# Releasing two granule loads by an average instead of a landed transpose, and moving the fourth block product by one step

## The chip, the cores and the metric

The kernel runs on one core of a Trainium2 chip. The core has a matrix engine (PE, with PEld for its weight loads), a vector engine (DVE), a scalar engine (ACT), GpSimd (POOL) and SyncE (SP, which here only issues transfers), and 16 DMA engines that move data between the device memory, called HBM in the profile, and the on-chip memory. Matrix results go to a small accumulation memory (PSUM) in which the kernel keeps pools of tiles. The metric is the device time of one execution in microseconds; lower is better.

## The reference

Attention with a sliding window and a few global keys, followed by a two-layer network. Shapes: batch 4, 8 heads, 768 positions, head size 64; the network has 3072 tokens, 512 features and 2048 hidden units.

```python
scores = scale * q @ k.T
keep = is_global | is_local            # 8 global keys, window of 96
scores = where(keep, scores - slope[h] * dist, -1e9)
a = softmax(scores);  x = a @ v        # x becomes 3072 x 512
h = x @ w_in
g = s * relu(h) ** 2 + b
out = g @ w_out
```

## The kernel before

**Granules and steps.** The 3072 tokens are cut into 12 granules of 256 tokens (two blocks of 128), three to a batch element. The attention of a granule is four units, one for each pair of heads. A *step* `s` (`step`, L956) handles units 2s and 2s+1, so granule j has the steps 2j and 2j+1. A step issues the score matmuls of step s+1 and their exponentials (ACT) and masks (DVE), then `stage_A` for its own two units: the average over the values on PE (L492), and the normalisation on DVE (reciprocal L462, product L463), which writes `xn[j]`. Between these it runs three lists of other work, `c0`, `c1` and `c2`, and a list `pre` ahead of the masks. The order on every engine is the order of the program text (`manual_schedule`); each engine works through its own queue, and waits come from the data and from tiles that are used again.

**From attention to the network.** When a granule's last step is done, `finish_granule(j)` (L947) turns `xn[j]` into `xT[j]`. From granule 4 on this is done by two DMA transposes from SP (L596). Then `hold_loads` (L120) puts a copy of one element on POOL, the *gate*: POOL's queue goes on only when that element is there. Behind it `load_granule(j + 4)` (L110) issues six loads of 128 KB on POOL (keys and queries into `nat`, L116, values into `vb`, L117, two blocks each; they cast from float32 to bf16). The keys and queries of granule j+2 are turned by DMA transposes as well (`qk_by_dma`, L357), which SP issues in the first of the two steps of granule j.

**The network.** The first matrix product of a granule is eight groups of 8 matmuls (`p1_mm`, L616), two groups to a *unit* `u1(j, q)`, q = 0 to 3: 16 matmuls of 128x256, a relu of each group (ACT, L626) and one square of the unit (ACT L792 or DVE L790). The second product of granules 4 to 11 is done for pairs (e, o) of granules with seven block products instead of eight (`product`, L816): sums and differences of hidden blocks (`g_sum`, L779) are multiplied by sums and differences of blocks of `w_out` (`weight_sums`, L750 to L753), and the results are joined on DVE (`evac` L825, `join` L864) and stored from SP. Each block product is 16 matmuls of 128x256, eight for each of the granule's two token blocks. The product numbers 1 to 7 name the operands; product 4 multiplies the second half of granule o's hidden units by the last weight difference, `t4`, which `weight_sums[3]` (L753) makes.

**The loop around the change.** The loop over pairs `pr` (L1149 to L1183) gives each pair four steps, from `k0 = 2e + 5`. In the kernel before, the third step runs the products 5 and 6, half sums, then product 4 (whose result is left in PSUM), then unit 0 of the next pair's granule e+2. The fourth step evacuates product 4 before the masks, runs product 3, and then units 1, 2 and 3 of granule e+2. `weight_sums[3]` closes the second step of the first such pair. The last pair (`tail`) has other lists in its third step.

**PSUM tiles of the network.** Products, `p1_mm` groups and others take tiles in turn from one pool of three (`ps_h`); a group or product can start when the result that lay in its tile three tiles ago has been read out. `stage_A` has a pool of one (`ps_av`).

Of the kernel before, what the change touches and what calls it, by code (L numbers as in the profile page):

```python
# [17 lines left out]
def kernel(  # L18
# [19 lines left out]
    DM = H * D  # L38
    DF = moe_w_in.shape[1]
    GB = 2  # L40
    GT = GB * P
# [78 lines left out]
    def hold_loads(ap):  # L120
        g = work.tile([P, 1], BF16, name="gate", tag="gate")
        nc.gpsimd.tensor_copy(g[0:1, :], ap)  # L122
# [144 lines left out]
    xn = {}  # L267
    xT = {}
# [324 lines left out]
    def x_by_dma(j):  # L593
        t = xT_tile(j)
        for i in range(GB):
            nc.sync.dma_start_transpose(t[:, :, i * P : (i + 1) * P], xn[j][:, i, :])  # L596
# [116 lines left out]
    def moe_p2_cols(j, tb, parts):  # L713
# [35 lines left out]
    weight_sums = [  # L749
        lambda: nc.vector.tensor_tensor(t1, w12, w11, ALU.subtract),  # L750
        lambda: nc.vector.tensor_tensor(t2, w22, t1, ALU.subtract),
        lambda: nc.vector.tensor_tensor(t3, w22, w12, ALU.subtract),
        lambda: nc.vector.tensor_tensor(t4, w21, t2, ALU.subtract),  # L753
    ]
# [3 lines left out]
    def quarter(j, half, c=None):  # L758
        lo, n = (0, NH) if c is None else (c * NH // 2, NH // 2)
        return g_of(j)[:, half * NH + lo : half * NH + lo + n, :]  # L760

    def g_sum(pr, n, c=None):

        def go():
            if pr not in gs_cur:
                gs_cur[pr] = [
                    gpool.tile([P, NH, GT], BF16, name="gsum", tag=f"gsum{i}", bufs=1)
                    for i in range(4)
                ]
            e, o = 2 * pr, 2 * pr + 1  # L770
            cs = slice(0, NH) if c is None else slice(c * NH // 2, (c + 1) * NH // 2)
            s1, s2, s3, s4 = (t[:, cs, :] for t in gs_cur[pr])
            dst, x, y, op = {
                1: (s1, quarter(o, 0, c), quarter(o, 1, c), ALU.add),
                2: (s2, s1, quarter(e, 0, c), ALU.subtract),
                3: (s3, quarter(e, 0, c), quarter(o, 0, c), ALU.subtract),
                4: (s4, quarter(e, 1, c), s2, ALU.subtract),
            }[n]
            nc.vector.tensor_tensor(dst, x, y, op)  # L779

        return go

    def unit_p1(j, q):

        for fp in (2 * q, 2 * q + 1):
            relu, _ = p1_mm(j, fp)
            relu()
        gs = g_of(j)[:, 4 * q : 4 * q + 4, :]
        if j % 2 or q == 3:
            outs.append(lambda: nc.vector.tensor_tensor(gs, gs, gs, ALU.mult))  # L790
        else:
            nc.scalar.activation(gs, gs, ACT.Square)  # L792
# [4 lines left out]
    def product(pr, n, tbs=range(GB), ps=None, cols=None):  # L797

        j = 2 * pr
        stat = {  # L800
            1: lambda: quarter(j, 0),
            2: lambda: quarter(j, 1),
            3: lambda: gs_cur[pr][3],
            4: lambda: quarter(j + 1, 1),
            5: lambda: gs_cur[pr][0],
            6: lambda: gs_cur[pr][1],
            7: lambda: gs_cur[pr][2],
        }[n]()
        mov = {1: w11, 2: w21, 3: w22, 4: t4, 5: t1, 6: t2, 7: t3}[n]
        cs = slice(0, CH) if cols is None else cols  # L810
        if ps is None:
            ps = ps_h.tile([P, GB, CH], F32, name="ps_2", tag="psh")
        prod_ps[pr, n] = ps
        for tb in tbs:
            for fc in range(NH):
                nc.tensor.matmul(  # L816
                    ps[:, tb, cs],
                    lhsT=stat[:, fc, tb * P : (tb + 1) * P],
                    rhs=mov[:, fc, cs],
                    start=(fc == 0),  # L820
                    stop=(fc == NH - 1),
                )

    def scaled(dst, ps, add):
        nc.vector.scalar_tensor_tensor(  # L825
            out=dst, in0=ps, scalar=s_bc[:], in1=add, op0=ALU.mult, op1=ALU.add
        )
# [6 lines left out]
    def both_blocks(ap):  # L834
        return ap.unsqueeze(1).to_broadcast((P, GB, CH))

    def put(pr, row, col, o, tb=None, c0=0, eng=nc.sync):

        b, g = divmod(2 * pr + row, NGR)
        t0 = b * S + g * GT  # L840
        cs = slice(col * CH, (col + 1) * CH)
        if tb is not None:
            t0 += tb * P
            c0 += col * CH
            eng.dma_start(out[t0 : t0 + P, c0 : c0 + o.shape[-1]], o)
        else:
            nc.sync.dma_start(out[t0 : t0 + GT, cs].rearrange("(a p) c -> p a c", p=P), o)
# [3 lines left out]
    def out_tile():  # L851

        n_out[0] += 1
        tag, bufs = (("first", 4), ("o_sb", 3))[n_out[0] % 2]
        return work.tile([P, GB, CH], F32, name="o_q", tag=tag, bufs=bufs)

    def store(pr, row, col, ps, add):

        o = out_tile()
        scaled(o[:].rearrange("p a c -> p (a c)"), ps, add)  # L860
        put(pr, row, col, o[:])

    def add_f32(dst, x, y):
        nc.vector.tensor_tensor(dst, x, y, ALU.add)  # L864

    def evac(pr, n):

        ps3 = prod_ps[pr, n][:]
        ps = ps3.rearrange("p a c -> p (a c)")
        if n == 1:  # L870
            res[pr] = [
                work.tile([P, GB, CH], F32, name=f"part{i}", tag=f"part{i}", bufs=1)
                for i in range(3)
            ]
            res[pr].append(out_tile() if pr == NJ // 2 - 1 else res[pr][0])
        r0, r1, r7, r6 = (t[:].rearrange("p a c -> p (a c)") for t in res[pr])
        if n == 1:
            scaled(res[pr][0][:], ps3, both_blocks(bvec[:, 0:CH]))
        elif n == 2:
            store(pr, 0, 0, ps, r0)  # L880
        elif n == 5:
            scaled(res[pr][1][:], ps3, both_blocks(bdiff[:]))
        elif n == 6:
            scaled(r6, ps, r0)
        elif n == 7:
            nc.scalar.activation(r7, ps, ACT.Copy, scale=s_bc[:])
        elif n == 3:
            store(pr, 0, 1, ps, r1)
        elif n == 4:
            store(pr, 1, 0, ps, r6)  # L890

    def join(pr, n):

        def go():
            _, r1, r7, r6 = (t[:].rearrange("p a c -> p (a c)") for t in res[pr])
            if n == 1:
                add_f32(r1, r1, r6)
            elif n == 0:
                add_f32(r6, r6, r7)
            else:  # L900
                o = out_tile()
                add_f32(o[:].rearrange("p a c -> p (a c)"), r7, r1)
                put(pr, 1, 1, o[:])

        return go

    def pe(pr, n):

        def go():
            product(pr, n)  # L910
            outs.append(lambda: evac(pr, n))

        return go

    def prod(pr, n):
        return lambda: product(pr, n)

    def u1(j, q):
        return lambda: unit_p1(j, q)

# [26 lines left out]
    def finish_granule(j):  # L947
        if j < X_PE:
            x_by_pe(j)
        else:  # L950
            x_by_dma(j)
        if 6 <= j + LEAD < NJ:
            hold_loads(xT[j][0:1, 0, GT - 1 : GT])
            load_granule(j + LEAD)

    def step(s, c0, c1, c2, pool=None, pre=()):  # L956
# [192 lines left out]
    for pr in range(2, NJ // 2):  # L1149
        e, o = 2 * pr, 2 * pr + 1  # L1150
        k0 = 2 * e + 5
        if k0 >= NU // 2:
            break
        step(
            k0,
            [pe(pr, 2)],
            [u1(o, 0)],
            [u1(o, 1), flush, g_sum(pr, 3, 0)],
            pre=[pe(pr, 1), flush],
        )  # L1160
        step(
            k0 + 1,
            [u1(o, 2)],
            [u1(o, 3), g_sum(pr, 1, 0)],
            [g_sum(pr, 1, 1), pe(pr, 7), g_sum(pr, 2)] + [weight_sums[3]] * (pr == 2),
            pre=[g_sum(pr, 3, 1)],
        )
        tail = k0 + 3 >= NU // 2
        step(
            k0 + 2,  # L1170
            [u1(e + 2, 0), pe(pr, 5)] if tail else [pe(pr, 5), flush, pe(pr, 6)],
            [pe(pr, 6), g_sum(pr, 4, 0)] if tail else [g_sum(pr, 4, 0), prod(pr, 4)],
            [g_sum(pr, 4, 1), u1(e + 2, int(tail)), join(pr, 1)],
        )
        if tail:
            break
        step(
            k0 + 3,
            [u1(e + 2, 1)],
            [join(pr, 2), u1(e + 2, 2)],  # L1180
            [u1(e + 2, 3)],
            pre=[join(pr, 0), lambda: evac(pr, 4), pe(pr, 3), flush],
        )  # L1183
    join(pr, 0)()
    for n in (3, 4):
# [4 lines left out]
    e, o = 2 * pr, 2 * pr + 1  # L1190
# [50 lines left out]
```

## Time and profile before

| | |
|---|---|
| median of 4 runs | 209.59 us (209.21, 209.48, 209.70, 209.76) |
| the profiled execution | 209.23 us, span 207.5 us |
| PE busy | 201.2 us (97%), granted clock 1.00 |
| DVE, ACT, POOL busy | 160.6, 128.5, 69.1 us |
| DMA | 28.17 MB in 110308 packets, of which 97836 under 512 bytes |
| queue of POOL's loads (q0) | 75472 packets, 13.11 MB |
| queue of SP's transfers (q1) | 33612 packets, 14.13 MB |
| transposes of xT, issue to landing | shortest 2.4, median 4.5, longest 9.2 us |

The page gives busy times and their shares by engine, then the span in 40 slices with the busy share in tenths, the chain of work that ended last, and the costliest groups of instructions. `L816` is line 816 of the kernel; `out<-in` names tiles. A matmul's duration in the profile includes the time in which it overlaps with the next one, so the pace of a run of matmuls is read from their starts. The steps of the first pair begin near 94.3, 102.4, 108.9 and 117.1 us, those of the second near 125.3, 133.4, 139.6 and 147.8 us.

### The profile page before, as it was taken

The page shows a single profiled execution, that of the slowest core. Times are in us where ns is not written, and L with a number is a line of the kernel's source. Part 1 is how long each engine was busy: PE and PEld are TensorE (multiplying, and loading weights), DVE is VectorE, ACT ScalarE, POOL GpSimd, SP SyncE. Part 2 cuts the span into 40 slices and gives each one's busy share as a digit, 9 for nine tenths or more (in the row PEclk, how much of TensorE's full clock was granted, in tenths as well). Part 3 has the DMA queues.
Part 4 walks back from the last instruction along what each step waited for, and adds up shares of the span by engine and source line. Part 5 has one row for each costly group of instructions (what it writes and reads, how often), then busy time and mean ns, then how long its engine had stood idle before and what let it go on. Part 6 is the DMA issues. An engine that isn't in the chain of part 4 may idle for free.

```text
span 207.5 us, 5323 instructions
## 1 busy us (share of the span) xinstructions
PE 201.2 (97%) x2191; PEld 159.9 (77%) x2191; DVE 160.6 (77%) x336; ACT 128.5 (62%) x200; POOL 69.1 (33%) x89
## 2 busy tenths in 40 slices
PE   6899999999999999999999999999999999999993
PEld 2677884556876685878888898888898889888883
DVE  7685689995989955799799974699865696737974
ACT  4975669484975648786564595664695764476200
POOL 8994244999737102703800917300000000000000
PEclk9999999999999999999999999999999999999999
DMA  6999999999999999999999999996460300240006
GB/s 166 171 180 206 206 208 174 155 152 136 118 149 153 155 159 173 93 240 247 140 207 130 126 145 178 205 202 79 53 205 3 89 17 0 52 153 0 0 6 200
DMA packets 110308, 28.17 MB, mean 136 GB/s; under 512 B 97836, under 2 KB 108780, under 8 KB 110284
## 3 DMA queue, kind: packets, MB, share of 16 engines
q0 software_dynamic: 75472, 13.11, 86.5%
q1 hardware_dynamic: 33612, 14.13, 39.4%
q10 hardware_dynamic: 1200, 0.59, 1.1%
q8 instruction: 17, 0.28, 0.6%
q14 instruction: 7, 0.06, 0.1%
HBM read 27.26 MB, written 6.29 MB: 162 GB/s over the span
## 4 chain that ended last, share of the span: by engine, by line
PE 82%; DMA 13%; POOL 4%; issue 0%; DVE 0%; POOLq 0%
PE ps L616 34%; PE ps L816 24%; PE ps L664 13%; DMA w_out_bf<-in_moe_w_out_dram 9%; PE ps_s L438 5%; PE ps_av L492 5%; DMA w_in_bf<-in_moe_w_in_dram 3%; POOL nat L102 2%; POOL vb L108 1%; PE ps_t L348 1%; PE ps_last L816 0%; PE ps_x L588 0%; POOL w_in_bf L140 0%; DVE o_last L825 0%; POOL rel L173 0%
## 5 line engine op out<-in xcount | busy, mean ns | idle before, releaser
L616 PE MATMUL ps<-xT,w_in_bf 128*128 128x256 bf16 x768 | 90.4, 273 | 0.5 <-DMA w_in_bf<-in_moe_w_in_dram 0.5
L626 ACT ACTIVATE gT<-ps 128x512 bf16<-128x512 f32 x96 | 55.7, 598 | 47.4 <-PE ps L616 47.1
L616 PEld LDWEIGHTS <-w_in_bf 128*128 128x128 bf16 x768 | 72.9, 98 | 10.0 <-DMA w_in_bf<-in_moe_w_in_dram 0.7
L447 ACT ACTIVATE pt<-ps_s 128x1024 bf16<-128x1024 f32 (+1 forms) x44 | 39.3, 946 | 3.1 <-PE ps_s L438 3.1
L664 PE MATMUL ps<-w_out_bf,gT 128*128 128x512 bf16 x128 | 29.8, 380 | 0.2 <-DMA w_out_bf<-in_moe_w_out_dram 0.2
L816 PEld LDWEIGHTS <-gsum 128*128 128x128 bf16 x256 | 24.2, 98 | 3.7 <-DVE gsum L779 0.5
L454 DVE TENSOR_TENSOR pt<-pt,tmpl 128x1024 bf16<-128x1024 bf16 (+1 forms) x40 | 24.5, 644 | 1.7 <-ACT pt L447 1.6
L790 DVE TENSOR_TENSOR gT<-gT 128x1024 bf16<-128x1024 bf16 x20 | 13.7, 687 | 11.7 <-ACT gT L626 11.7
L664 PEld LDWEIGHTS <-gT 128*128 128x128 bf16 x128 | 11.7, 98 | 13.5 <-issue 0.5
L463 DVE TENSOR_TENSOR xn<-ps_av,rc 128x256 bf16<-128x256 f32 x48 | 20.4, 425 | 1.7
L816 PEld LDWEIGHTS <-gT 128*128 128x128 bf16 x200 | 18.6, 98 | 2.3
L117 POOL DMA_DIRECT2D vb<-in_v_dram x20 | 18.2, 910 | 6.5 <-DMA nat<-in_k_dram 2.9
L116 POOL DMA_DIRECT2D nat<-in_k_dram x20 | 17.7, 886 | 7.9 <-DMA w_in_bf<-in_moe_w_in_dram 2.7
L116 POOL DMA_DIRECT2D nat<-in_q_dram x20 | 17.8, 891 | 6.7 <-DMA vb<-in_v_dram 2.5
L462 DVE RECIPROCAL rc<-ps_av 128x4 f32<-128x4 f32 x48 | 8.9, 186 | 12.2 <-PE ps_av L492 10.2
L492 PEld LDWEIGHTS <-pt 128*128 128x128 bf16 x320 | 14.4, 97 | 2.7 <-DVE xn L463 0.7
L629 DVE TENSOR_TENSOR gT<-gT 128x512 bf16<-128x512 bf16 x32 | 12.9, 420 | 3.6 <-ACT gT L626 3.3
L492 PE MATMUL ps_av<-vb,pt 128*128 128x65 bf16 x208 | 15.4, 193 | 0.0
L816 PE MATMUL ps<-w_out_bf,gsum 128*128 128x256 bf16 x128 | 15.3, 273 | 0.0
L816 PE MATMUL ps<-wsub,gsum 128*128 128x256 bf16 x128 | 15.1, 273 | 0.0
L122 POOL COPY gate<-xT 1x1 bf16<-1x1 bf16 x6 | 1.4, 237 | 40.0 <-DMA xT<-xn 38.9
L816 PE MATMUL ps<-w_out_bf,gT 128*128 128x256 bf16 x120 | 13.9, 273 | 0.0
(112 smaller groups left out, 222.6 us busy)
## 6 DMA issues: line engine op xcount, KB each, us to landing
out_dram<-o_q SPq DMA_DIRECT2D x15, 256.0 KB, 2.4
vb<-in_v_dram POOLq DMA_DIRECT2D x24, 128.0 KB, 7.4
nat<-in_k_dram POOLq DMA_DIRECT2D x22, 128.0 KB, 6.7
nat<-in_q_dram POOLq DMA_DIRECT2D x22, 128.0 KB, 7.3
w_out_bf<-in_moe_w_out_dram POOLq DMA_DIRECT2D x4, 512.0 KB, 17.2
w_in_bf<-in_moe_w_in_dram POOLq DMA_DIRECT2D x3, 512.0 KB, 11.0
out_dram<-o_sb SPq DMA_DIRECT2D x4, 256.0 KB, 6.0
out_dram<-o_early SPq DMA_DIRECT2D x4, 256.0 KB, 5.6
```

The costliest lines, as they stand in the source:

```text
L116: nc.gpsimd.dma_start(t[:, n, i, :, :], rows_of(srcs[n], b, sb))
L117: nc.gpsimd.dma_start(vbuf[b % 2][:, sb, :, 0:D], rows_of(v, b, sb))
L447: nc.scalar.activation(pt[:, :, 0:ncol], ps[:, :, 0:ncol], ACT.Exp, scale=QSCALE)
L454: nc.vector.tensor_tensor(pv, pv, m.rearrange("p h a c -> p h (a c)"), ALU.mult)
L463: nc.vector.tensor_tensor(dst, av[:, :, :, 0:D], rc[:].to_broadcast((P, 2, 2, D)), ALU.mult)
L492: nc.tensor.matmul(av[:, i, hi, 0 : D + 1], lhsT=pt[:, hi, c * P : (c + 1) * P], rhs=vv, start=(n == 0), stop=(n == len(terms) - 1),)
L616: nc.tensor.matmul(ps[:, i, :], lhsT=w_in_bf[:, kc, fc * P : (fc + 1) * P], rhs=xT[j][:, kc, :], start=(kc == 0), stop=(kc == KC - 1),)
L626: nc.scalar.activation(gs, ps[:], ACT.Relu)
L629: nc.vector.tensor_tensor(gs, gs, gs, ALU.mult)
L664: nc.tensor.matmul(po[:], lhsT=g_of(j)[:, fc, tb * P : (tb + 1) * P], rhs=w_out_bf[:, fc, :], start=(fc == 0), stop=(fc == FC - 1),)
L790: outs.append(lambda: nc.vector.tensor_tensor(gs, gs, gs, ALU.mult))
L816: nc.tensor.matmul(ps[:, tb, cs], lhsT=stat[:, fc, tb * P : (tb + 1) * P], rhs=mov[:, fc, cs], start=(fc == 0), stop=(fc == NH - 1),)
```

## The change

The gate of the loads that follow granules 4 and 5, those of granules 8 and 9, now copies an element of `xn` that the last normalisation writes, instead of an element of `xT` that the second transpose lands. The later gates stay on `xT`.

In the third step of a pair, unit 0 of granule e+2 moves from the end to the place of product 4, and unit 1 comes where unit 0 was. Product 4 goes to the fourth step, after product 3, with its evacuation issued like that of other products. The last weight subtraction moves from the end of the second step to the end of the third one, behind the join.

```diff
@@ finish_granule
         if 6 <= j + LEAD < NJ:
-            hold_loads(xT[j][0:1, 0, GT - 1 : GT])
+            if j in (4, 5):
+                hold_loads(xn[j][0:1, GB - 1, DM - 1 : DM])
+            else:
+                hold_loads(xT[j][0:1, 0, GT - 1 : GT])
             load_granule(j + LEAD)
@@ the loop over pairs, second step
-            [g_sum(pr, 1, 1), pe(pr, 7), g_sum(pr, 2)] + [weight_sums[3]] * (pr == 2),
+            [g_sum(pr, 1, 1), pe(pr, 7), g_sum(pr, 2)],
             pre=[g_sum(pr, 3, 1)],
@@ third step
             [u1(e + 2, 0), pe(pr, 5)] if tail else [pe(pr, 5), flush, pe(pr, 6)],
-            [pe(pr, 6), g_sum(pr, 4, 0)] if tail else [g_sum(pr, 4, 0), prod(pr, 4)],
-            [g_sum(pr, 4, 1), u1(e + 2, int(tail)), join(pr, 1)],
+            [pe(pr, 6), g_sum(pr, 4, 0)] if tail else [g_sum(pr, 4, 0), u1(e + 2, 0)],
+            [g_sum(pr, 4, 1), u1(e + 2, 1), join(pr, 1)] + [weight_sums[3]] * (pr == 2),
@@ fourth step
-            [u1(e + 2, 1)],
+            [pe(pr, 4)],
             [join(pr, 2), u1(e + 2, 2)],
             [u1(e + 2, 3)],
-            pre=[join(pr, 0), lambda: evac(pr, 4), pe(pr, 3), flush],
+            pre=[join(pr, 0), pe(pr, 3), flush],
```

The helper `prod(pr, n)`, which issued a product without its evacuation, is removed with its only use.

More of the change, by code (lines that the diff above doesn't have):

```diff
@@ L913, in pe @@
         return go
-    def prod(pr, n):
-        return lambda: product(pr, n)
     def u1(j, q):
```

## The prediction

> **What bounds the kernel now.** I read the page first (parts 1, 2 and 4), then the busy time by stage, then the chain in order of time where the diff touches the code, then the timeline of the gates, and last what the DMA queues moved beside each other.
>
> The page of the kernel before, parts 1, 2 and 4:
>
> ```profile
> PE 201.2 (97%) x2191; PEld 159.9 (77%) x2191; DVE 160.6 (77%) x336; ACT 128.5 (62%) x200; POOL 69.1 (33%) x89
> ...
> DMA  6999999999999999999999999996460300240006
> ...
> PE 82%; DMA 13%; POOL 4%; issue 0%; DVE 0%; POOLq 0%
> ```
>
> The matrix engine is busy for 97% of the span and carries 82% of the chain that ended last. The DMA part of the chain is the loading of weights before 34.7 us. The DMA engines are busy, too, until about slice 28 of 40 (145 us). The busy time by stage (window; its length, then busy us and instructions of PE, PEld, DVE, ACT, POOL; granted clock; DMA share; GB/s):
>
> ```profile
> 76.00:94.00 18.00, 18.00 (x188) 12.75 (x186) 13.86 (x32) 14.10 (x26) 5.43 (x7) 1.00 1.58 178
> 94.00:126.00 32.00, 32.00 (x387) 27.44 (x385) 27.24 (x50) 20.77 (x30) 11.40 (x15) 1.00 1.63 164
> ```
>
> In both stages that the diff touches PE has no idle time, at a granted clock of 1.00. The chain there (start, us, what):
>
> ```profile
> 109.51 3.72 PE ps L816 x32
> 113.23 0.24 PE ps_av L492 x8
> 113.47 1.75 PE ps L816 x16
> 115.22 0.24 PE ps_av L492 x8
> 115.46 1.75 PE ps L616 x16
> 117.21 0.55 PE ps_s L438 x16
> 117.76 1.85 PE ps L816 x16
> 119.61 1.75 PE ps L616 x16
> ```
>
> This is the third step of the first pair (from 108.95 us) and the start of its fourth. A product of 16 matmuls and one unit of the first MoE product of 16 matmuls take the same 1.75 us, or 109 ns a matmul. So PE runs back to back: what is exchanged on it costs nothing, and the change can gain only where PE waits. The starts of successive matmuls show all that is lost between 96 and 170 us: about 0.08 us at 100.5, 0.14 at 106.6, 0.11 at 109.8, 0.05 at 137.4, 0.18 at 140.4 and 0.14 at 168.2, in all 0.7 us. Each is in a place whose instructions the diff leaves as they are.
>
> The gates, from the timeline (start, us, engine and line; in brackets the idle time before and what ended it):
>
> ```profile
> 76.31 2.51 SPq L596 DMA_TRANSPOSE xT<-xn  x2
> 81.17 0.18 POOL L122 COPY gate<-xT 1x1 bf16<-1x1 bf16 x1 [12.10 <-DMA xT<-xn]
> 84.06 1.91 PE L616 MATMUL ps<-xT,w_in_bf 128*128 128x256 bf16 x16
> ...
> 96.89 0.53 POOL L122 COPY gate<-xT 1x1 bf16<-1x1 bf16 x1 [9.90 <-DMA xT<-xn]
> 98.50 1.91 PE L616 MATMUL ps<-xT,w_in_bf 128*128 128x256 bf16 x16
> ...
> 114.13 0.18 POOL L122 COPY gate<-xT 1x1 bf16<-1x1 bf16 x1 [11.39 <-DMA xT<-xn]
> 115.30 1.91 PE L616 MATMUL ps<-xT,w_in_bf 128*128 128x256 bf16 x16
> ```
>
> Each gate fires when xT of granules 4, 5 and 6 has landed, and PE needs that xT 2.9, 1.6 and 1.2 us later. These slacks are what the change spends or earns.
>
> **The change part by part.**
>
> 1. Loads of granules 8 and 9. The gate copy waits for the last normalise instead of the landing. For granule 4 that ends at 75.86 + 0.42 = 76.28 us, so the copy moves up from 81.17 by 4.9 us. For granule 5 SyncE issues the first transpose at 90.07, right behind the last normalise, so the gate opens at about 90.1, 6.8 us sooner. On POOL's queue behind the gate are only the six loads (0.88 to 0.92 us each, 5.3 us from 81.74 to 87.0) and the next gate. No other engine waits for the gate. The xn buffers turn over three granules later, so the new read of xn blocks nobody.
>
> What the early loads collide with is the price. The transposes of xT4 are issued at 76.31, behind a store, and now share the DMA engines with granule 8 loads. With both queues full, and with transposes alone (two windows of 1 us):
>
> ```profile
> q1 hardware_dynamic: 412, 0.11, 78.7%
> q0 software_dynamic: 412, 0.05, 78.2%
> ...
> q1 hardware_dynamic: 942, 0.23, 121.9%
> ```
>
> These are 73 to 74 us and 80 to 81 us. A transpose moves 128 KB, so it takes 0.13/0.11 = 1.2 us in company and 0.13/0.23 = 0.55 us alone. In the old run the first data of a load flows about 2 us after its issue (issue 81.74, first packets near 83.7), so granule 8 now flows from about 79, just where granule 7 ends. Two transposes at 1.2 instead of 0.55 us make xT4 1.3 us later: 82.4 instead of 81.1, against a need at 84.06. It stays covered, by 1.6 us. The bounds: nothing, and the longest transpose of the run, 9.2 us from issue to landing (xT's issues: 2.4, median 4.5, 9.2). The second issue, near 77.6, would then land at 86.8 and stall PE by 2.8 us. I take zero, because the 1.2 us row is from the stretch just before and of the same kinds of packets.
>
> The transposes of granule 7's keys and queries come next (issued 78.9 to 85.3, needed by the scores at 94.33): 5 us in company, covered. xT5 (issued at 90.07) stood behind four stores and the rest of granule 8's loads. Those loads now finish near 88, granule 9's first data come at 90.1 + 0.6 + 2 = 92.7, and between them the stores have the engines to themselves (92 to 93 us: 0.29 MB of q1 in 1 us). I put xT5 at 94 to 97, against the need at 98.50: zero, with up to 0.7 us if it takes 2.4 us more than now. xT6 (issued at 102.70) stood among granule 9's loads, issued 97.5 to 102.7. These are now nearly done at 102.7, so xT6 should land near 107 to 109, not 114.1. Granule 10's loads, still gated by it, move up with it.
>
> 2. The third step takes unit 0 and then unit 1 of granule e+2, and the fourth product goes to the fourth step (pairs 2 and 3; the last pair's lists are unchanged). PE: 16 matmuls of 109 ns against 16 of 109 ns, zero. The new demand is xT6 at 113.3 instead of 115.3, covered by 4 to 6 us if item 1 holds. If xT6 came as late as now, PE would wait 114.1 - 113.3 = 0.8 us. The second pair's unit starts at about 144 instead of 145.9, and its xT was issued from 132.5: even 9.2 us later it is there.
>
> ACT: two relus (0.60 each) and a square (1.06) move into its 4.86 us of idle time before 116.37. They end near 116.9, so the next two relus and the square run up to 0.6 us later and the exponentials of the fourth step 0.3 us later. Masks and average that use them come a step later. Zero.
>
> PSUM (three buffers in turn): unit 0 takes the buffers of products 7 and 5, which DVE and ACT free about 1 us before. In the fourth step unit 3 takes product 4's buffer, freed when its evacuation (0.75 us) ends. Scores at 117.2, masks until about 121.75 (ACT ends them), normalise until 122.4, evacuation until 123.15; unit 3 starts at 123.4 to 123.6. The nearest row is the first step of the same pair, where the same order costs 0.08 us at 100.45. I take 0, bound 0.2 us in each of two pairs.
>
> 3. The last weight subtraction (one DVE instruction, 1.22 us at 111.12) moves behind the joins of the third step. DVE gets 1.22 us before the masks at 112.25, where PE waits for nothing, so no gain. It now ends near 118.7, and product 4 reads it at 119.5: covered by 0.7 us; without that cover PE would wait at most its own length, 1.2 us, once. The evacuation of product 4 moves too, one for one, and its store with it.
>
> One rule speaks against the moved loads. The rows first: POOL's issues took 0.88 to 0.92 us each from 81.7 to 87.0, while DVE was busy for 4.76 of the 5 us from 82 to 87. The Trainium skill, "SBUF — State Buffer", section "SBUF: two separate sides", says that descriptors of loads issued by GpSimd can't be written while VectorE holds the shared port in a two-port mode. By that rule six loads, each held by one 1.22 us operation, would come some 7 us later, and xT6 would land as late as now: an estimate from that page's mechanism of 0.8 us more. The rows show no such hold here, so it does not enter my sum.
>
> **Sum.** Profiled execution: 209.23 us, span 207.5 and 1.7 around it. The change: 0 (PE exchange) + 0 (xT4, xT5, xT6 covered) + 0 (evacuation, subtraction) = 209.23. The four runs have 209.21 to 209.76, median 209.59, that is 0.36 above the profiled one; the middle of that spread is 209.5, which I forecast.
>
> **The rivals.**
> - Slower: xT4 comes late. Place: unit 0 of granule 4 at 84.06. It decides as soon as the early loads hold the transposes for more than 2.9 us. For: the stretches 74.5 to 75.5 and 84.5 to 88 us, where both queues crawl for 1 us or more. Against: 1.3 us by the shared pace. One such crawl on top makes 0.2 us, a second 1.2, the bound 2.8. Time 210.2 to 212.3, typically 210.5. Chance 14%.
> - Slower: xT6 no sooner, because the loads of granule 9 are held elsewhere. Then 0.8 us at 113.3, or 210.3. For: xT6 needs two transposes behind two stores. Against: the loads have left the queue by then. The half case, in which the change doesn't do what it says for the loads, is the same. Chance 6%.
> - Faster: other executions than the profiled one lose time at xT6, whose slack is only 1.2 us, and the change gives it 4 to 6. The most that this can bring is back to the fastest run, 209.2, and with the 0.08 us at 100.45 (DVE's evacuation, no longer beside POOL's issues) 209.1. Against: the 0.36 us may as well come from the weight loads before 34.7. Chance 10% to pass 0.2%.
>
> **How the numbers follow.** Unchanged, as PE has no gap to close: 70%. A measurement of this kernel can tell about 0.2% (0.42 us) from no change. Slower 20% (14 + 6), faster 10%. The likeliest case alone is 209.1 to 209.9. Up to 210.7 the range takes in xT6 late and most of xT4 late; down to 208.8 the faster case with the spread of runs. Outside lie the worst of xT4 and what I have not seen, about one in ten.
>
> **What would show it.** Right: gates near 76.5 and 90.3; PE busy for all of 76 to 126 us; xT4 landed before 84, xT6 before 111; unit 0 of granule 6 at about 113.3; the subtraction near 117.5 on DVE; granule 10's gate (xT6 landed) before 111. Wrong: PE idle before line 616 near 84, 98.5 or 113.3, or before line 616 near 123.5 for want of the buffer that DVE frees.

## The result, and the profile after

The changed kernel takes 210.01 us in the median of 39 runs (209.40 to 212.15), the kernel before 209.53 us in the median of 61 (209.06 to 210.15). The ratio is 1.0033, with a 95% interval of 1.0024 to 1.0042: slower by 0.24 to 0.42%. The forecast was no change. The spread grew with it: the slowest run of before lies 0.6 us above its median, that of after 2.1 us. The ratios leave out executions more than 1.5% above the fastest of their kernel; there is one, of 214.37 us.

The profiled execution took 210.22 us, span 208.4. The same parts of its page:

```profile
PE 201.6 (97%) x2191; PEld 160.0 (77%) x2191; DVE 160.7 (77%) x336; ACT 128.6 (62%) x200; POOL 69.4 (33%) x89
...
DMA  5999999999999999999998999996451210240006
...
PE 74%; DMA 16%; POOL 4%; DVE 3%; SPq 1%; issue 1%; POOLq 0%
```

DMA has grown from 13 to 16% of the chain that ended last and SyncE's queue has entered it. The two stages of after (columns as before):

```profile
76.00:94.00 18.00, 18.00 (x188) 12.77 (x186) 13.77 (x31) 14.10 (x26) 10.07 (x13) 1.00 1.72 196
94.00:126.00 32.00, 31.55 (x375) 27.16 (x373) 27.84 (x52) 20.39 (x30) 8.13 (x11) 1.00 1.62 162
```

PE, which had no idle time in either stage, now has 0.45 us of it in the second. In the first the DMA engines moved 196 instead of 178 GB/s: the early loads add to what is moved there. Where the 0.45 us lies is shown by the chain of after:

```profile
90.44 0.04 issue
90.48 1.22 SPq L596
91.70 0.05 issue
91.75 7.69 DMA xT<-xn
99.44 0.05 issue
99.49 1.92 PE ps L616 x16
```

The second transpose of granule 5 is issued at 91.75 and lands 7.69 us later, at 99.44; PE needed it at about 98.9. In the kernel before it was issued at 91.37 and landed at 96.77, 5.4 us later. The timeline of after, gates and the starts of PE's units:

```profile
76.77 0.31 POOL L122 COPY gate<-xn 1x1 bf16<-1x1 bf16 x1 [7.19 <-DVE xn L463]
89.43 0.57 POOL L122 COPY gate<-xn 1x1 bf16<-1x1 bf16 x1 [6.81 <-DVE xn L463]
99.49 1.70 PE L616 MATMUL ps<-xT,w_in_bf 128*128 128x256 bf16 x14 [0.41 <-DMA xT<-xn]
111.64 0.58 POOL L122 COPY gate<-xT 1x1 bf16<-1x1 bf16 x1 [16.33 <-DMA xT<-xn]
```

Both gates open about when the forecast said, 4.4 and 7.5 us sooner than before; xT6 lands at 111.5, 2.5 us sooner. But PE waits for xT5. From the starts of the matmuls the gap there is 0.58 us, and a gap of 0.08 us right behind it in the kernel before (100.4) is gone. This and a growth of 0.06 us in the gap near 107 make 0.55 us of the 0.97 us between the two spans. Another 0.35 us is a gap near 45 us, before any instruction that the change moves; it comes and goes between executions of several of the kernels below, so a single profile has to be read place by place, not by its time. It stands in five of the seven profiled executions of kernels with the new order in the first pair, and in none of the five others; whether that is chance, no run here tells.

What took the time from xT5 is seen in the queues. The last 4 us before it lands in the kernel before (93 to 97 us), q1 being SyncE's queue with stores and transposes, q0 POOL's loads:

```profile
q1 hardware_dynamic: 1398, 0.82, 92.1%
q0 software_dynamic: 1034, 0.13, 50.5%
```

and the last 4.5 us in the changed kernel (95 to 99.5 us):

```profile
q0 software_dynamic: 3199, 0.40, 159.7%
q1 hardware_dynamic: 900, 0.38, 49.1%
```

SyncE's queue moved 0.21 MB per us before and 0.08 after. Granule 9's loads took the place.

### The profile page after: what moved, and what is told of

Same layout as the page of the kernel before. It is cut to its first block, busy times and chain, and to the rows that moved or that the text cites. A ratio compares the mean times of both kernels' runs of the same rounds, so it can differ in the third digit from the quotient of the medians.

```text
span 208.4 us, 5323 instructions
## 1 busy us (share of the span) xinstructions
PE 201.6 (97%) x2191; PEld 160.0 (77%) x2191; DVE 160.7 (77%) x336; ACT 128.6 (62%) x200; POOL 69.4 (33%) x89
## 4 chain that ended last, share of the span: by engine, by line
PE 74%; DMA 16%; POOL 4%; DVE 3%; SPq 1%; issue 1%; POOLq 0%
PE ps L616 32%; PE ps L816 22%; PE ps L664 10%; DMA w_out_bf<-in_moe_w_out_dram 9%; PE ps_av L492 4%; DMA w_in_bf<-in_moe_w_in_dram 4%; PE ps_s L438 4%; DMA xT<-xn 4%; POOL nat L102 2%; POOL vb L108 1%; PE ps_t L348 1%; DVE wsum L642 1%; SPq L596 1%; DVE pt L454 1%; PE ps_last L816 0%
## 5 line engine op out<-in xcount | busy, mean ns | idle before, releaser
L792 ACT ACTIVATE gT<-gT 128x1024 bf16<-128x1024 bf16 x12 | 12.7, 1057 | 0.4
```

## The experiments

Theory A: the time is lost wherever a granule's xT lands after PE wants its first unit. The early loads of granule 9 do that to xT5, and they earn nothing back but cover for xT6, which the new order needs 2 us sooner. Theory B: granule 8's early loads are enough to make xT5 late. Theory C: the new order of the steps costs the time.

**One part at a time: only granule 8's gate moved, with the new order.**

```diff
-            if j in (4, 5):
+            if j == 4:
```

> The changed kernel, but only granule 8's loads (behind granule 4) are released by the average; granule 9's loads wait for the landed transpose of granule 5 again. Theory A (granule 9's loads, released at 89 to 90 us, push the transposes of granule 5 past the 98.5 us at which PE needs them): xT5 lands near 96 to 97.5, no PE gap before its first unit, ratio to before 0.999 to 1.001. Theory B (granule 8's loads delay the stores and key transposes that lie ahead of xT5 in SP's queue, and that alone makes it late): the gap near 98.5 stays, 0.3 to 0.6 us, ratio 1.002 to 1.004. Theory C (the new order of the third and fourth step costs the time): ratio 1.002 to 1.004 with no gap at 98.5.

Measured: 209.88 us, ratio 1.0015 (1.0005 to 1.0025). xT5 landed at 94.99 and its first unit started at 99.11; xT6 landed at 112.91, with its first unit at 113.97. PE has no gap at either:

```profile
98.92 0.35 PE L492 MATMUL ps_av<-vb,pt 128*128 128x65 bf16 x6
99.11 1.91 PE L616 MATMUL ps<-xT,w_in_bf 128*128 128x256 bf16 x16
```

Theory B falls: with granule 8 early and granule 9 not, xT5 lands no later than in the kernel before (96.77). The ratio is above what A expected, and this execution does not lose its time at an xT: its span is 0.65 us longer than that of the kernel before, and by the last normalisation of granule 4, near 76 us, 0.6 us of this is there already, some 0.3 at the gap near 45 us. Whether other executions lose theirs in such places or at xT6, which had 1.1 us to spare, is open.

**Only granule 9's gate moved, with the new order.**

```diff
-            if j in (4, 5):
+            if j == 5:
```

> The changed kernel, but only granule 9's loads (behind granule 5) are released by the average; granule 8's loads wait for the landed transpose of granule 4. Theory A: granule 8's loads now still run at 90 us and granule 9's follow at once, so xT5 is as late as in the changed kernel or later: gap at 98.5 of 0.5 us or more, ratio 1.002 to 1.006. Theory B: no gap at 98.5, ratio 0.999 to 1.001. Theory C: ratio 1.002 to 1.004 without that gap.

Measured: 209.69 us (209.30 to 211.54), ratio 1.0016 (0.9998 to 1.0034). xT5 landed at 98.49, just ahead of its use at 98.75, xT6 at 113.74 with a gap of 0.15 us before its first unit. The gap of 0.5 us that A expected was not in this execution, and the interval does not exclude no loss. What it tells is the landing: xT5 1.7 us later than in the kernel before, where only granule 9's gate differs ahead of it. In the four executions of kernels with both gates as before, xT5 landed between 95.98 and 96.77.

**The gates alone, in the old order.** The edit is the gate hunk of the change on the kernel before.

```diff
-            hold_loads(xT[j][0:1, 0, GT - 1 : GT])
+            if j in (4, 5):
+                hold_loads(xn[j][0:1, GB - 1, DM - 1 : DM])
+            else:
+                hold_loads(xT[j][0:1, 0, GT - 1 : GT])
```

> Only the two early gates; the order of the steps is that of the kernel before. Theories A and B: the gap at 98.5 us is there as in the changed kernel, 0.3 to 0.7 us with a tail to 2 us in single runs, ratio 1.002 to 1.004. Theory C: no loss, ratio 0.999 to 1.001.

Measured: 210.04 us, ratio 1.0031 (1.0018 to 1.0043), as in the changed kernel. Its profile caught the execution of 214.37 us; what that one shows stands in the last section. A second execution was profiled:

> A second look at the kernel with only the two early gates, whose first profile was of an execution far longer than its others. Theory A: again a gap before the first unit of granule 5 near 98.5 to 99 us, 0.3 to 1.2 us at a time of 209.7 to 210.6, and none before granule 6, whose xT lands near 111 against a need at 115.3 to 116.

That execution took 209.99 us. xT5 landed at 99.23 and PE stood before it, by its matmul starts for 0.82 us; the timeline:

```profile
99.28 1.64 PEld L616 LDWEIGHTS <-w_in_bf 128*128 128x128 bf16 x16 [0.77 <-DMA xT<-xn]
99.28 1.92 PE L616 MATMUL ps<-xT,w_in_bf 128*128 128x256 bf16 x16 [0.65 <-DMA xT<-xn]
```

xT6 landed at 111.98 against a first use at 116.06. So the gates by themselves cost what the whole change costs, and the loss is at xT5.

**The order alone, all gates as before.**

```diff
-            if j in (4, 5):
+            if j in ():
```

> Only the new order of the third and fourth step; all gates wait for landed transposes as before. Theory A: xT5 lands near 96.8 and there is no gap at 98.5, but xT6 lands near 114 while its first unit is due at 113.3, so a gap of 0.5 to 1.0 us there and a ratio of 1.002 to 1.005. If the order by itself costs nothing and xT6 happens to land sooner, the ratio is 1.000. Theory C: ratio 1.002 to 1.004 with the loss in evacuations near 116 to 124 us and none before 113.3.

Measured: 210.41 us (209.55 to 211.55), ratio 1.0043 (1.0026 to 1.0061): the largest loss of all. The profile was of an execution of 209.59 us without a gap there: xT6 landed at 113.15 and was used at 113.68. Hence a second execution:

> A second look at the kernel with only the new order; its first profile was of one of its shortest executions and showed xT6 landing 0.5 us before its use. Theory A: in an execution of 210 us or more, PE stands before the first unit of granule 6 near 113.5 until xT6 lands, for about what the execution is longer than 209.6; in one near 209.6 there is no such gap. Theory C: a longer execution shows its loss elsewhere, near 116 to 125 us.

This one took 210.6 us. xT6 landed at 114.56, and its gate and PE's unit go together:

```profile
114.69 0.18 POOL L122 COPY gate<-xT 1x1 bf16<-1x1 bf16 x1 [12.38 <-DMA xT<-xn]
114.70 1.47 PE L616 MATMUL ps<-xT,w_in_bf 128*128 128x256 bf16 x12 [0.83 <-DMA xT<-xn]
```

By the matmul starts the gap is 1.00 us, and the two executions of one kernel differ by 1.01 us: the difference is here. No new gap follows near 116 to 125. The wait rests on one late part of the landing (last section): the rest of xT6 was in by 112.91, 0.8 us before PE wanted it.

**The order in the second pair alone,** where xT8 has time to spare; gates and subtraction as before.

```diff
+        new = pr == 3 and not tail
...
-            [pe(pr, 6), g_sum(pr, 4, 0)] if tail else [g_sum(pr, 4, 0), prod(pr, 4)],
-            [g_sum(pr, 4, 1), u1(e + 2, int(tail)), join(pr, 1)],
+            [pe(pr, 6), g_sum(pr, 4, 0)] if tail else [g_sum(pr, 4, 0), u1(e + 2, 0) if new else prod(pr, 4)],
+            [g_sum(pr, 4, 1), u1(e + 2, int(tail or new)), join(pr, 1)],
...
-            [u1(e + 2, 1)],
+            [pe(pr, 4) if new else u1(e + 2, 1)],
...
-            pre=[join(pr, 0), lambda: evac(pr, 4), pe(pr, 3), flush],
+            pre=[join(pr, 0)] + ([] if new else [lambda: evac(pr, 4)]) + [pe(pr, 3), flush],
```

> The kernel before with the new order of the third and fourth step in the second pair alone, whose xT (granule 8's) lands near 139 against a first use near 144; gates and the weight subtraction as before. Theory A (the order costs only because xT6 isn't there at 113.3): ratio 0.9985 to 1.0007, no gap near 144 to 155. Rival C (the order itself costs, by the square on the scalar engine, the PSUM tiles or the evacuations): about half of the loss of the order alone, ratio 1.0015 to 1.003.

Measured: 209.54 us, ratio 0.9999 (0.9990 to 1.0008). xT8 landed at 140.71, its first use was at 144.35. The stage by the view of busy times (a PE of 18.98 in 19 us):

```profile
138.00:157.00 19.00, 18.98 (x228) 16.17 (x227) 14.87 (x29) 12.41 (x18) 0.00 (x0) 1.00 0.71 121
```

Theory C falls for the order as such: in the second pair, where xT is there, it costs nothing.

**Granule 8's gate in the old order.** The edit is that of the gates alone, with `if j == 4`.

> The kernel before with one edit: granule 8's loads are released by the average, granule 9's by the landed transpose. Theory A (each xT late for its first unit is what costs): xT5 lands near 95 against a need at 98.5 to 99, xT6 near 113 against 115.3 to 116, no gap at either: ratio 0.9985 to 1.0005. Rival (early loads of granule 8 cost PE something by themselves, by way of the vector engine or of other transfers): ratio 1.001 to 1.003, with PE gaps between 84 and 110 us that the kernel before doesn't have.

Measured: 209.54 us, ratio 0.9999 (0.9989 to 1.0010). The early loads of granule 8 cost nothing by themselves. xT5 landed at 96.80 and xT6 at 114.06, not at 95 and 113 as expected; both were in time (98.72 and 115.57).

**xT5 one store further ahead, in the changed kernel.** Of the four early stores, the third (256 KB) now goes to SyncE behind xT5's transposes and the value copies.

```diff
-        late[2:4] + [shifted_copy, weight_sums[0]],
+        [shifted_copy] + late[2:4] + [weight_sums[0]],
```

> The changed kernel with both early gates and the new order; one list of the step at 82 to 88 us starts with the template copy, so that the third of the four early stores (256 KB) is issued behind xT5's transposes and not ahead of them. Theory A, with its mechanism (xT5 stands in SP's queue behind stores that share the DMA engines with the early loads): xT5 lands 1 to 2 us sooner, 97.5 to 98.5, the gap at 98.5 to 99 shrinks from 0.58 us to 0 to 0.2, xT6 stays near 111.5; ratio 0.9995 to 1.002. Rival (the loads slow the transposes themselves, wherever they stand in the queue): xT5 still lands at 99 or later, ratio 1.002 to 1.004.

Measured: 209.69 us (209.17 to 210.04), ratio 1.0008 (0.9999 to 1.0017), against 1.0033 for the changed kernel, with no run above 210.04. xT5 landed at 95.62 instead of 99.44, used at 98.55; xT6 at 109.68. The timeline of PE where the gap was, and of the gate on xT6:

```profile
98.36 0.35 PE L492 MATMUL ps_av<-vb,pt 128*128 128x65 bf16 x6
98.55 1.91 PE L616 MATMUL ps<-xT,w_in_bf 128*128 128x256 bf16 x16
...
109.80 0.27 POOL L122 COPY gate<-xT 1x1 bf16<-1x1 bf16 x1 [14.85 <-DMA xT<-xn]
```

Against the second execution of the changed kernel (below; like this one it lacks the gap near 45 us) xT5 was issued 1.0 us sooner, at 89.09 instead of 90.08, as SyncE no longer stood at a store that waits for DVE, and landed 3.1 us sooner than its 98.75. This is more than expected. The rival, that the loads slow the transposes wherever they stand in the queue, falls as it was stated. The loads do slow them: here the second transpose landed 1.9 us behind the first (93.70), in the kernel before 0.6 us behind it. The place in SyncE's queue decides together with the company.

**The changed kernel once more.**

> A second look at the changed kernel. Theory A: time above 209.2 us is the PE gap before the first unit of granule 5 near 98.9 us (xT5 landing at 98.9 plus that gap), plus 0.35 us where the gap near 45 us, long before the change, is there too; no gap before granule 6 near 113.5 to 114.3, with xT6 landed before 112.5. Rival: a gap elsewhere between 100 and 125 us.

The execution took 209.50 us: xT5 landed at 98.75, a gap of 0.28 us by the matmul starts before its first unit at 98.79; xT6 landed at 111.30, used at 113.59. No gap near 45 us in this one.

The landings and first uses side by side (us; the second transpose's landing, the start of the first unit; from one execution each):

| kernel | ratio | xT5 lands, used | xT6 lands, used |
|---|---|---|---|
| before | 1 | 96.77, 98.50 | 114.01, 115.30 |
| changed | 1.0033 | 99.44, 99.49 | 111.51, 114.29 |
| changed, second execution | | 98.75, 98.79 | 111.30, 113.59 |
| gates alone, second execution | 1.0031 | 99.23, 99.28 | 111.98, 116.06 |
| order alone, second execution | 1.0043 | 96.33, 98.90 | 114.56, 114.70 |
| xT5 ahead | 1.0008 | 95.62, 98.55 | 109.68, 113.40 |

Each kernel here with a ratio of 1.003 or more has a row in which landing and use stand 0.04 to 0.14 us apart: there PE had waited. The two ratios near 1.0015, of one early gate with the new order, are not explained by waits for xT in their profiles.

No version beat the kernel before: PE runs there almost without a gap, so the most that the experiments could do was to return to it.

## Why the prediction was wrong, point by point

**The bound** was right: PE is all but gapless in the kernel before, an exchange on it is worth nothing (0.9999 for the order in the second pair), and only a new wait could move the time.

**Item 1, xT5, is the step that failed.** It put the landing at 94 to 97 us and the cost at zero, with a bound of 0.7. It landed at 99.44 and 98.75 in two executions, for gaps of 0.58 and 0.28 us. What it said of the stores held. Granule 8's data had flowed by about 89 us, though its last landing came at 91.6, and from 90 to 93.8 us the stores had the engines to themselves:

```profile
q1 hardware_dynamic: 612, 1.02, 73.4%
q0 software_dynamic: 3, 0.00, 0.2%
```

The last store ahead of xT5 landed at 94.65, in the kernel before at 95.20. (It could have been sooner: from 90.0 to 91.2 us the DMA engines moved almost nothing, at most 11 GB/s, and the cause of that is open.) The term that failed is the two transposes behind the stores. Granule 9's data flowed from 93.8 us, so the transposes ran in their company, and the second landed 4.8 us after the last store (4.2 us in the other execution) instead of 1.6 us in the kernel before. The forecast named no time for company in xT5's own transposes. Its price for that, 1.2 us each, read from a single 1 us and used for xT4, would still have put xT5 at about 97, in time; in the changed kernel the second transpose of xT4 and of xT5 landed 1.9 to 2.4 us behind the first.

One reading was wrong too: SyncE's issue at 90.07 was not right behind the last normalisation of granule 5, which had ended at 88.88; SyncE had stood at a store that waits for DVE. So granule 9's gate opened 1.05 us ahead of the first transpose's issue (89.43 and 90.48) and not with it. The bound of 0.7 us covers both profiled executions of the changed kernel, but not its runs up to 212.15 us.

**Item 1, xT4:** forecast 82.4, measured 83.7 against a use at 84.47. It was right that it stays covered, but the forecast was 1.3 us too early; the slack left was 0.8 us, half of what I had.

**Item 1, xT6:** forecast 107 to 109, measured 111.5. The direction was right, the size about half: 2.5 us sooner, not 5 to 7. Granule 9's loads were not nearly done at 102.7; the last of them landed at 107.44. And 1.7 of the 2.5 us are one late part of the landing in the kernel before (last section); the rest of xT6 moved only from 112.31 to 111.50.

**Item 2, order:** zero on PE, ACT and PSUM was right. I named the price of a late xT6, 0.8 us, as a rival at 6% in which the loads fail to help. The order alone shows that price as a gap of 1.00 us in the longer of its two profiled executions. The loads paid it, and made the other gap.

**Item 3, subtraction:** zero, right: no new gap between 113 and 126 us in the changed kernel.

**The rule on the vector engine's lock.** POOL's early issues took 0.88 to 0.92 us each in the changed kernel as well, and behind 75 us no profile here has one above 0.94. So none of these issues shows the hold that the Trainium skill's page "SBUF — State Buffer" (section "SBUF: two separate sides") describes. Only some one-element gate copies grew, to 0.31 to 0.58 us, where most of before had 0.18 and one 0.53; why, no run here tells.

**The rivals.** The slower side had 20%, through xT4 and xT6; the mechanism was theirs, but the place was xT5, between the two, which I had cleared. Its slack in the kernel before, 1.6 us, was hardly more than xT6's 1.2.

## What to carry to other kernels

When an engine is gapless, moving transfers forward can only pay where something waits, and it spends the slack of everything that shares the DMA engines: list each such landing with its slack, and check the early transfers against all of them, above all those behind stores in the same queue. Price a transpose beside loads from a stretch of several microseconds: here a row of 1 us gave 1.2 us, and 1.9 to 2.4 us were measured. Two edits that cover for each other have to be tried apart: here each lost by itself (1.0031 and 1.0043) and the pair lost 1.0033, since the loads that rescued one transpose delayed the one before it. A transfer's place in its queue counts as much as its company: one store moved behind the transposes brought them in some 3 us sooner.

## What the runs showed of the hardware that was not expected

**A gap in PE can cost more than its length.** The first profile of the gates alone is of an execution of 214.37 us. xT5 landed at 102.02 there, PE stood idle for about 2.7 us, and then ran a unit at half speed (columns as in the other views of stages):

```profile
98.50:102.00 3.50, 0.87 (x13) 0.69 (x10) 2.81 (x6) 0.00 (x0) 0.00 (x0) 1.00 1.62 206
102.06:105.40 3.34, 3.34 (x16) 2.40 (x17) 0.00 (x0) 0.60 (x1) 0.00 (x0) 0.50 1.58 170
105.40:108.00 2.60, 2.60 (x40) 2.10 (x37) 1.21 (x3) 1.63 (x3) 0.00 (x0) 1.00 1.38 183
```

The granted clock is 1.00, then 0.50 for 3.3 us, then 1.00 again; in the middle row the matmuls start 213 ns apart instead of 109. The 2.7 us gap cost some 1.7 us more (16 x 104 ns). The gaps of up to 1.0 us in the other profiles were followed by matmuls at 109 ns. The Trainium skill, "TensorE: Matmul & The Clock Gate", Part 1, puts the fall to half rate after an idle window of about 3.4 us; here 2.7 us of idle time was followed by it, in one execution.

**One part of a landing can come long after the others.** The trace counts each landing in sixteen parts. Of the second transpose of xT6 in the kernel before, fifteen were in by 112.31 us and the last at 114.01. Between 113.3 and 113.8 us the DMA engines moved next to nothing, so this wait is not for granule 9's loads:

```profile
q1 hardware_dynamic: 20, 0.01, 8.4%
```

The last part came 1.6 to 1.7 us behind the fifteenth in all seven profiled executions of kernels with at most one early gate, and with the others in all five with both. In the execution of 214.37 us it happened to xT5: fifteen parts were in by 100.64 and the last at 102.02, which makes half of PE's 2.7 us. What holds the part back is not shown.
